# Chunked attention and expert layer on one core: two heads' key rows interleaved, memory values added by a product

## The chip, the core and the metric

The kernel runs on one core of one Trainium2 chip. The metric is the device time of one execution in microseconds (us), as the median of several runs. One execution is also recorded by the hardware profiler; all views of the profile below come from that one.

The core has a matrix engine (PE, which multiplies a loaded weight tile by a moving operand and writes into the accumulator memory, PSUM), a vector engine (DVE), a scalar engine (ACT), a general engine (POOL, which here also issues most of the DMAs) and a queue engine (SP, which only issues DMAs). The working memory has 128 partitions. The engines run on their own and wait for one another by semaphores.

## The reference

Two layers follow each other. The first is attention with a short window: batch 4, 8 heads, 768 positions, head size 64. The positions are cut into chunks of 32; each chunk sees its own 32 keys, 16 to the left and 8 to the right, so 56, and 8 memory keys that all chunks of a head share, 64 in all.

```python
for c in range(nc):
    q_c = q[:, :, c_start:c_end]
    k_full = np.concatenate([mem_k, k_ctx], axis=2)
    v_full = np.concatenate([mem_v, v_ctx], axis=2)
    scores = scale * np.matmul(q_c, k_full.transpose(0, 1, 3, 2))
    scores = scores - np.max(scores, axis=-1, keepdims=True)
    a = np.exp(scores)
    a = a / (np.sum(a, axis=-1, keepdims=True) + 1e-09)
    out[:, :, c_start:c_end] = np.matmul(a, v_full)
```

The second layer sends each of the 3072 resulting rows of 512 numbers to 2 of 8 experts, chosen by noisy logits (`x @ w_gate` plus noise scaled by a softplus of `x @ w_noise`). Each expert computes `np.maximum(x @ w1[e], 0) @ w2[e]` with a hidden width of 1024, and the two results are added with softmax weights.

## The kernel before

**Stages.** The attention works through the four batches one after the other. Within a batch it takes 256 queries at a time, two tiles of 128, so there are 3 iterations per batch and 12 in all (index i, or t in the helpers). Beside it, groups of finished rows are routed (the class `Route`: logits to choices, ranks and lists), and at the end the lists are decoded. Then comes the experts' stage: it gathers rows by pairs of experts and computes the expert layers in `mm1` (L697) and `mm2` (L709). The attention's working buffers (`xrow`, `vn`, `vb`, `nat`) lie in the place of experts' weights that are loaded later.

**Values' home.** `vb[b % 2]` holds, for each of the 24 chunks of a batch, the values that its queries see, in a layout for two heads at once. Partitions 0 to 63 belong to the even head of a pair: first its 8 memory rows, then its 56 key rows. Partitions 64 to 127 belong to the odd head in the same way. In the free direction there are two halves, `a = 0` for even heads and `a = 1` for odd heads. The even heads' partitions hold values in half 0 and zeros in half 1, the odd heads' the other way round, so that one product over 128 partitions gives both heads' results side by side. The zeros are written once: for `vb[1]` by ACT (L218), for `vb[0]` by DVE (L515).

How it is filled, per batch: the values `vn` (loaded by POOL, L117) are put in order by two POOL copies into `vp` (`spread_v`, L357). SP writes `vp` to the buffer `vd` in main memory (L363). POOL then issues six DMAs (`window_v`): two bring the 8 memory rows of the batch from `mvn` into the partitions of each head, copied for all 24 chunks (L367), and four bring the 56 key rows of each head, 32 and 24 rows at a time (L372). `mvn` comes from four SP loads of `mem_v` (L162) and a DVE cast (L516).

**An iteration.** `scores(i + 1)`: PE multiplies the queries by the memory keys (8 products over the whole array, L397) and by the windows' keys (32 products, each in one quarter of the array's columns, L404). DVE takes the maximum (L412) and subtracts it (L414); ACT takes the exponentials into `pb` (`exps`, L419). `turn_p(i)`: PE transposes `pb` in 8 pieces (L425), so that a pair of heads lies over the partitions with its 2 x 64 keys, and ACT copies the result to `pT` (L428). `turn_x(i - 1)`: PE transposes the finished rows (L459), ACT copies them (L461). `values(i)`: 8 products with the two columns of `ones2` give the sums of the exponentials (L436), into the PSUM tile `small`; 32 products in quarters of the array give the weighted values (L442), into `ps_o`. DVE takes the reciprocal of the sums (L446) and multiplies by it, once per tile of 128 queries (L449). `gate(i - 1)`: PE multiplies the transposed rows by the router's weights (L469), into other columns of `small`, and DVE copies the logits out (L471). Between these, `fill` transposes the next batch's keys and queries (L382) and copies them (L536); before the loop the same helper's copies for batch 0 are at L521.

**What sets the order.** The attention loop stands in a block of manual schedule for PE, ACT, DVE and SP: each engine works in the order in which the program writes its instructions. POOL's instructions keep their order by `pin`. So an instruction that waits holds back all that stands behind it on its engine. Waits are put in by the framework from the use of the tiles. PSUM is given out as three buffers that take turns for transposes (`psT`), one for `ps_s`, one for `ps_o` and one for `small`.

The loop's order, from the program:

```python
            if not last:
                sc = scores(i + 1)
            pTs[i] = turn_p(pbs.pop(i))
            if i:
                keep_x(i - 1, nc.scalar)
                xTs_[i - 1] = turn_x(xrs.pop(i - 1))
            fill(i, 1)
            xrs[i] = values(i, pTs.pop(i), (lambda: gate(i - 1, xTs_.pop(i - 1))) if last else None)
            if last:
                break
            pbs[i + 1] = exps(sc)
            ...
            if i:
                gate(i - 1, xTs_.pop(i - 1))
```

Of the kernel before, what the change touches and what calls it, by code (L numbers as in the profile page):

```python
# [22 lines left out]
def kernel(  # L23
# [29 lines left out]
    NCH = S // CH  # L53
# [6 lines left out]
    const = ctx.enter_context(tc.tile_pool(name="const", bufs=1))  # L60
# [3 lines left out]
    w_all = wpool.tile([128, E, WE], BF16, name="w_all")  # L64
# [5 lines left out]
    def pin(i):  # L70
        tc.keep_in_program_order(i)
# [23 lines left out]
    NP = len(pairs)  # L95
# [13 lines left out]
    vb = [scratch(2 * NCH * HP * D).rearrange("p (a c w) -> p a c w", a=2, c=NCH) for _ in range(2)][::-1]  # L109
    nat = [[scratch(H * SO * D).rearrange("p (h c) -> p h c", h=H) for _ in range(2)] for _ in range(2)]  # L110
    assert scol[0] >= 2 * WE
    mvs = w_all[0:B * NM, 0, 0:2 * H * D].bitcast(F32).rearrange("p (h d) -> p h d", h=H)

# [15 lines left out]
    actx = ExitStack()  # L129
# [5 lines left out]
    psO = actx.enter_context(tc.psum_pool(name="psO", bufs=1))  # L135
    psG = actx.enter_context(tc.psum_pool(name="psG", bufs=1))

# [22 lines left out]
    nc.vector.tensor_copy(mkn, mks)  # L160
    for b in range(B):
        nc.sync.dma_start(out=mvs[b * NM:(b + 1) * NM], in_=mem_v[b].rearrange("h m d -> m h d"))  # L162
    mvn = keep.tile([B * NM, Dm], BF16, name="mvn")
    wgs = keep.tile([128, KP, 2 * E], F32, name="wgs")
# [6 lines left out]
                   allow_small_or_imprecise_dtypes=True)  # L171

    ones2 = const.tile([128, 2], BF16, name="ones2")
    nc.vector.memset(ones2, 0.0)
    nc.vector.memset(ones2[0:64, 0:1], 1.0)
    nc.vector.memset(ones2[64:128, 1:2], 1.0)


# [20 lines left out]
    nc.gpsimd.iota(facts[:, :, 1], pattern=[[1, NG]], base=1, channel_multiplier=0, allow_small_or_imprecise_dtypes=True)  # L199

    ohp = const.tile([128, NG, NP], BF16, name="ohp")
    rank = const.tile([128, NG], F32, name="rank")
# [5 lines left out]
    def bc(ap, n):  # L208
        return ap.unsqueeze(len(ap.shape)).to_broadcast(list(ap.shape) + [n])

    def own(par):
        return slice(par * 64, par * 64 + 64)
# [4 lines left out]
    for par in range(2):  # L217
        nc.scalar.copy(vb[1][own(par), 1 - par].rearrange("p (x c) w -> p x (c w)", x=NCH // 2),  # L218
                       zeros[own(par), :].unsqueeze(1).to_broadcast([64, NCH // 2, Dm]))

# [140 lines left out]
    def window_v(b):  # L361
        t, o = vb[b % 2], vd[b % 2]
        nc.sync.dma_start(out=o[LC:LC + S, :].rearrange("(p s) c -> p (s c)", s=SO), in_=vp)  # L363
        for par in range(2):
            p0 = par * 64
            cols = slice(par * 256, (par + 1) * 256)
            pin(nc.gpsimd.dma_start(out=t[p0:p0 + NM, par], in_=mvn[b * NM:(b + 1) * NM, cols].unsqueeze(1).to_broadcast([NM, NCH, 256])))  # L367
        for par in range(2):
            p0 = par * 64
            cols = slice(par * 256, (par + 1) * 256)  # L370
            for r0, n in ((0, CH), (CH, WIN - CH)):
                pin(nc.gpsimd.dma_start(out=t[p0 + NM + r0:p0 + NM + r0 + n, par],  # L372
                                        in_=o[r0:r0 + S, cols].rearrange("(c k) w -> k c w", k=CH)[0:n]))

# [13 lines left out]

    small = psG.tile([128, 4, 128], F32, name="small")

# [26 lines left out]
    def exps(sc):  # L417
        pb = work.tile([128, 2 * HP, 2, KW], BF16, name="pb")
        nc.scalar.activation(out=pb.rearrange("p x a w -> p (x a) w"), in_=sc, func=Act.Exp, scale=scale)  # L419
        return pb  # L420

    def turn_p(pb):
        p_p = bank([128, 2 * HP, 128], BF16, name="p_p")
        for x in range(2 * HP):
            nc.tensor.transpose(out=p_p[:, x, :], in_=pb[:, x].rearrange("p a w -> p (a w)"),  # L425
                                identity=identb)
        pT = work.tile([128, 2 * HP, 128], BF16, name="pT")
        nc.scalar.copy(pT, p_p)  # L428
        return pT

    def values(t, pT, between=None):
        b, tp = divmod(t, TP)
        ps_g = small[:, t % 2, 0:2 * H].rearrange("p (j h) -> p j h", j=2)
        for x in range(2 * HP):
            j, pair = divmod(x, HP)
            nc.tensor.matmul(out=ps_g[:, j, 2 * pair:2 * pair + 2], lhsT=pT[:, x, :], rhs=ones2,  # L436
                             start=True, stop=True)
        ps_o = psO.tile([128, 2, HP, 2, D], F32, name="ps_o")
        for j in range(2):
            for pair in range(HP):  # L440
                for r in range(4):
                    nc.tensor.matmul(out=ps_o[r * CH:(r + 1) * CH, j, pair], lhsT=pT[:, j * HP + pair, r * CH:(r + 1) * CH],  # L442
                                     rhs=vb[b % 2][:, :, (tp * 2 + j) * 4 + r, pair * D:(pair + 1) * D],
                                     start=True, stop=True, tile_position=(0, r * CH))
        rs = work.tile([128, 2, H], F32, name="rs")
        nc.vector.reciprocal(rs, ps_g)  # L446
        xr = xrow[b % 2][:, 2 * tp:2 * tp + 2]
        for j in range(2):
            nc.vector.tensor_tensor(out=xr[:, j, 0:Dm].rearrange("p (h d) -> p h d", h=H),  # L449
                                    in0=ps_o[:, j].rearrange("p c a d -> p (c a) d"), in1=bc(rs[:, j], D), op=Alu.mult)  # L450
            if j == 0 and between is not None:
                between()
        return xr
# [10 lines left out]
    def gate(t, xT):  # L464
        b, tp = divmod(t, TP)
        ps_l = small[:, 2 + t % 2, 0:4 * E].rearrange("p (j e) -> p j e", j=2)
        for j in range(2):
            for kp in range(KP):
                nc.tensor.matmul(out=ps_l[:, j, :], lhsT=xT[:, kp, j, :], rhs=wgn[:, kp, :],  # L469
                                 start=(kp == 0), stop=(kp == KP - 1))  # L470
        nc.vector.tensor_copy(lg_all[:, 2 * t:2 * t + 2, :], ps_l)  # L471
# [34 lines left out]
    with tc.manual_schedule(engines={ET.PE, ET.Activation, ET.DVE, ET.SP}):  # L506
# [7 lines left out]
        for par in range(2):  # L514
            nc.vector.memset(vb[0][own(par), 1 - par], 0.0)  # L515
        nc.vector.tensor_copy(mvn.rearrange("m (a c d) -> m a c d", a=2, c=HP), mvs.rearrange("m (c a) d -> m a c d", a=2))  # L516
        spread_v(0)
# [9 lines left out]
        nc.vector.tensor_copy(wgn, wgs)  # L527
        pf = work.tile([128, 2, NP], F32, name="pf")
        sidon(pf, pab)
# [438 lines left out]
```

## Time and profile before

| what | value |
|---|---|
| median of 3 runs | 369.55 us (367.07 to 370.01) |
| profiled execution, its own time | 367.86 us |
| its span in the profile | 366.2 us |
| mean granted PE clock | 0.872 |
| PE, DVE, ACT, POOL busy | 282.3, 171.0, 136.7, 134.9 us |
| DMA moved | 56.97 MB in 55462 packets |
| vd windows, L372 | 8 DMAs of 384 KB, 8 of 288 KB |
| memory rows, L367 | 8 DMAs of 96 KB |

How to read the views: a line of a group or of a timeline has the start (timeline only), the busy time, the engine (PEld is PE's loading of weights), the program line, the operation, the tile written and, behind the arrow, the tiles read, and the shape; `x8` is the number of instructions that the line merges. In square brackets stands the idle time of the engine ahead of it and what ended that time; "issue" means that the profile shows nothing that it waited for. Buffers that lie in the experts' weights are all called `w_all` there. The windows view gives, for each stretch of time, its length, the busy time of each engine with the number of instructions, the granted PE clock as a share of full speed, the DMA share and GB/s. A POOL DMA line is the time to issue it, not to move its bytes.

### The profile page before, as it was taken

The page shows a single profiled execution, that of the slowest core. Times are in us where ns is not written, and L with a number is a line of the kernel's source. Part 1 is how long each engine was busy: PE and PEld are TensorE (multiplying, and loading weights), DVE is VectorE, ACT ScalarE, POOL GpSimd, SP SyncE. Part 2 cuts the span into 40 slices and gives each one's busy share as a digit, 9 for nine tenths or more (in the row PEclk, how much of TensorE's full clock was granted, in tenths as well). Part 3 has the DMA queues.
Part 4 walks back from the last instruction along what each step waited for, and adds up shares of the span by engine and source line. Part 5 has one row for each costly group of instructions (what it writes and reads, how often), then busy time and mean ns, then how long its engine had stood idle before and what let it go on. Part 6 is the DMA issues. An engine that isn't in the chain of part 4 may idle for free.

```text
span 366.2 us, 7045 instructions
## 1 busy us (share of the span) xinstructions
PE 282.3 (77%) x2941; PEld 181.3 (50%) x2941; DVE 171.0 (47%) x344; ACT 136.7 (37%) x189; POOL 134.9 (37%) x181
## 2 busy tenths in 40 slices
PE   0347373766817752599999999999989999999992
PEld 0236363555715641565554455764436675565540
DVE  7656274699766989431223300964300233312231
ACT  8714554463644360034333243222234223234310
POOL 6460473336435014742651453352480032201122
PEclk9995656685775885599999999999999999999997
DMA  8999999999999999379999999991299982100012
GB/s 115 247 155 169 248 162 155 258 199 199 237 176 198 228 225 180 80 147 179 159 186 206 250 184 240 101 215 54 69 154 186 193 185 80 52 2 2 24 43 81
DMA packets 55462, 56.97 MB, mean 156 GB/s; under 512 B 20119, under 2 KB 45783, under 8 KB 55424
## 3 DMA queue, kind: packets, MB, share of 16 engines
q0 software_dynamic: 34240, 46.82, 73.9%
q1 hardware_dynamic: 14048, 6.62, 9.5%
q10 hardware_dynamic: 7136, 3.02, 4.3%
q8 instruction: 25, 0.41, 0.5%
q14 instruction: 13, 0.11, 0.1%
HBM read 70.39 MB, written 13.96 MB: 230 GB/s over the span
## 4 chain that ended last, share of the span: by engine, by line
issue 25%; PE 21%; POOL 8%; DVE 5%; DMA 2%; POOLq 1%; ACT 0%; another core or an unknown queue 0%; DVEq 0%
PE p_h L697 10%; PE p_y L709 9%; POOL out_dram L660 6%; DMA out_dram<-y,main_dst 1%; POOL xt L654 1%; DMA xt<-xd,main_src 1%; PE p_xt L674 1%; DVE h L683 1%; POOL w_all L826 0%; DVE cum L322 0%; DVE w_all L449 0%; POOLq L963 0%; ACT xT L461 0%; DVE oh_l L328 0%
## 5 line engine op out<-in xcount | busy, mean ns | idle before, releaser
L709 PE MATMUL p_y<-w_all,h 128*128 128x512 bf16 x464 | 103.9, 379 | 1.5 <-ACT y L713 1.5
L697 PE MATMUL p_h<-xTt,w_all 128*128 128x256 bf16 (+3 forms) x672 | 102.9, 313 | 1.1 <-issue 0.5
L697 PEld LDWEIGHTS <-w_all 128*128 128x128 bf16 x736 | 69.8, 100 | 37.1 <-issue 1.6
L685 ACT ACTIVATE h<-p_h 128x512 bf16<-128x512 f32 (+1 forms) x81 | 44.5, 551 | 98.6 <-PE p_h L697 90.7
L709 PEld LDWEIGHTS <-h 128*128 128x128 bf16 x464 | 45.3, 98 | 53.2 <-issue 1.8
L683 DVE TENSOR_SCALAR h<-p_h 128x512 bf16<-128x512 f32 (+1 forms) x49 | 31.0, 632 | 85.9 <-PE p_h L697 70.5
L660 POOL DMA_INDIRECT out_dram<-y,main_dst x28 | 30.8, 1101 | 86.0 <-DVE y L715 75.6
L382 PE MATMUL p_t<-identb,w_all 128*64 128x128 bf16 x384 | 19.3, 272 | 30.8 <-DMA w_all<-in_k_dram 14.8
L715 DVE SCALAR_TENSOR_TENSOR y<-p_y,main_w,y 128x512 f32<-128x512 f32 x28 | 21.0, 750 | 37.9 <-PE p_y L709 33.3
L654 POOL DMA_INDIRECT xt<-xd,main_src x28 | 27.5, 982 | 26.3 <-DMA xTt<-xt 13.3
L713 ACT ACTIVATE y<-p_y,main_w 128x512 f32<-128x512 f32 x28 | 19.1, 687 | 38.8 <-PE p_y L709 35.6
L382 PEld LDWEIGHTS <-w_all 128*64 128x64 bf16 x384 | 16.4, 143 | 33.0 <-DMA w_all<-in_k_dram 15.5
L372 POOL DMA_DIRECT2D w_all<-vd x16 | 11.8, 745 | 26.4 <-DMA vd<-vp 25.3
L428 ACT COPY pT<-p_p 128x1024 bf16<-128x1024 bf16 x12 | 12.1, 1010 | 23.5 <-PE p_p L425 23.5
L449 DVE TENSOR_TENSOR w_all<-ps_o,rs 128x512 bf16<-128x512 f32 x24 | 15.5, 686 | 10.5 <-PE ps_o L442 10.0
L536 DVE COPY kT<-p_t 64x768 bf16<-64x768 bf16 x12 | 11.5, 955 | 12.5 <-PE p_t L382 12.4
L419 ACT ACTIVATE pb<-sc 128x1024 bf16<-128x1024 f32 x12 | 12.8, 1062 | 10.9 <-DVE sc L414 10.9
L357 POOL COPY vp<-w_all 128x1536 bf16<-128x1536 bf16 x8 | 11.5, 1467 | 13.3 <-DMA w_all<-in_v_dram 13.3
L442 PE MATMUL ps_o<-w_all,pT 128*32 128x128 bf16 x384 | 10.6, 274 | 6.1 <-issue 5.0
L412 DVE TENSOR_REDUCE mx<-ps_s 128x16 f32<-128x1024 f32 x12 | 14.7, 1223 | 1.2 <-PE ps_s L404 0.9
L414 DVE TENSOR_TENSOR sc<-ps_s,mx 128x1024 f32<-128x1024 f32 x12 | 14.7, 1224 | 0.8
L404 PE MATMUL ps_s<-kT,qT 128*32 128x112 bf16 x384 | 11.2, 274 | 3.6 <-DVE kT L536 2.4
(166 smaller groups left out, 279.3 us busy)
## 6 DMA issues: line engine op xcount, KB each, us to landing
w_all<-in_moe_w_dram POOLq DMA_DIRECT2D x16, 1024.0 KB
w_all<-in_moe_w_dram POOLq DMA_DIRECT2D x8, 512.0 KB
w_all<-in_v_dram POOLq DMA_DIRECT2D x4, 768.0 KB
w_all<-in_k_dram POOLq DMA_DIRECT2D x4, 768.0 KB
w_all<-in_q_dram POOLq DMA_DIRECT2D x4, 768.0 KB
vd<-vp SPq DMA_DIRECT2D x4, 768.0 KB, 6.9
w_all<-vd POOLq DMA_DIRECT2D x8, 384.0 KB
xd<-w_all ACTq DMA_DIRECT2D x11, 256.0 KB, 12.0
```

Of the source, the lines that this page charges most:

```text
L382: nc.tensor.transpose(out=p_t[own(par), s, :], in_=src[:, 2 * pair + par, s * D:(s + 1) * D], identity=identb, tile_position=(0, par * 64))
L412: nc.vector.tensor_reduce(out=mx, in_=s3, axis=AX, op=Alu.max)
L414: nc.vector.tensor_tensor(out=sc, in0=s3, in1=bc(mx, KW), op=Alu.subtract)
L449: nc.vector.tensor_tensor(out=xr[:, j, 0:Dm].rearrange("p (h d) -> p h d", h=H), in0=ps_o[:, j].rearrange("p c a d -> p (c a) d"), in1=bc( ...
L654: i = nc.gpsimd.indirect_dma_start(out=xts[key].bitcast(I32), out_offset=None, in_=xd, in_offset=bass.IndirectOffsetOnAxis(ap=ix, axis=0))
L660: i = nc.gpsimd.indirect_dma_start(out=out, out_offset=bass.IndirectOffsetOnAxis(ap=ix, axis=0), in_=y, in_offset=None, bounds_check=N - 1 ...
L683: nc.vector.tensor_scalar(out=out_, in0=in_, scalar1=0.0, scalar2=None, op0=Alu.max)
L685: nc.scalar.activation(out=out_, in_=in_, func=Act.Relu)
L697: nc.tensor.matmul(out=o, lhsT=w(kp * F + f * 128, 128), rhs=x[:, kp], start=(kp == 0), stop=(kp == KP - 1))
L709: nc.tensor.matmul(out=p, lhsT=h[:, (f * n + j) * 128:(f * n + j + 1) * 128], rhs=w(KP * F + f * Dm, Dm), start=(f == 0), stop=(f == FB - 1))
L713: nc.scalar.activation(out=y, in_=p, func=Act.Copy, scale=weight)
L715: nc.vector.scalar_tensor_tensor(out=y, in0=p, scalar=weight, in1=y, op0=Alu.mult, op1=Alu.add)
```

## The change

- In `vb`, the key rows of the two heads of a pair alternate: row r of the even head lies in partition 2 (8 + r), that of the odd head in the partition behind it. The exponentials `pb` are written with the heads alternating as well, so the transposed `pT` has the same order.
- The memory rows are no longer copied into `vb`. Its partitions 0 to 15 stay zero; so both halves of `vb` are zeroed over all 128 partitions.
- A new tile `mvz` holds, for each batch and pair, the memory values of both heads in partitions 0 to 15 (zeros below), 64 columns and a 65th per head; the 65th column is one in the partitions of the own head. Eight POOL DMAs fill it from `mem_v` at the start.
- In `values`, the product for the sums becomes a product with `mvz`, of 130 columns: it gives the memory part of both heads' results and the sums. The four window products of the same pair follow at once and add to it, so products over the whole array and in quarters of it alternate eight times.
- The PSUM tiles `ps_o` and `small` become one tile `prods` of 1536 columns. The parts of the two tiles of queries start at columns 0 and 703, the gate's results lie from 1408 on.
- The reciprocal is taken once per tile of 128 queries, ahead of each multiply.

```diff
-    mvs = w_all[0:B * NM, 0, 0:2 * H * D].bitcast(F32).rearrange("p (h d) -> p h d", h=H)
-    psG = actx.enter_context(tc.psum_pool(name="psG", bufs=1))
...
-    for b in range(B):
-        nc.sync.dma_start(out=mvs[b * NM:(b + 1) * NM], in_=mem_v[b].rearrange("h m d -> m h d"))
-    mvn = keep.tile([B * NM, Dm], BF16, name="mvn")
+    mvz = keep.tile([128, B, HP, 2, D + 1], BF16, name="mvz")
+    nc.vector.memset(mvz, 0.0)
...
-    ones2 = const.tile([128, 2], BF16, name="ones2")
...
+    for par in range(2):
+        for b in range(B):
+            pin(nc.gpsimd.dma_start(out=mvz[par:2 * NM:2, b, :, par, 0:D],
+                                    in_=mem_v[b].rearrange("(c a) m d -> a m c d", a=2)[par]))
...
-        nc.scalar.copy(vb[1][own(par), 1 - par].rearrange("p (x c) w -> p x (c w)", x=NCH // 2),
-                       zeros[own(par), :].unsqueeze(1).to_broadcast([64, NCH // 2, Dm]))
+        nc.scalar.copy(vb[1][:, par].rearrange("p (x c) w -> p x (c w)", x=NCH // 2),
+                       zeros.unsqueeze(1).to_broadcast([128, NCH // 2, Dm]))
...
-        for par in range(2):
-            p0 = par * 64
-            cols = slice(par * 256, (par + 1) * 256)
-            pin(nc.gpsimd.dma_start(out=t[p0:p0 + NM, par], in_=mvn[b * NM:(b + 1) * NM, cols].unsqueeze(1).to_broadcast([NM, NCH, 256])))
         for par in range(2):
-            p0 = par * 64
-            cols = slice(par * 256, (par + 1) * 256)
             for r0, n in ((0, CH), (CH, WIN - CH)):
-                pin(nc.gpsimd.dma_start(out=t[p0 + NM + r0:p0 + NM + r0 + n, par],
-                                        in_=o[r0:r0 + S, cols].rearrange("(c k) w -> k c w", k=CH)[0:n]))
+                p0 = 2 * (NM + r0) + par
+                pin(nc.gpsimd.dma_start(out=t[p0:p0 + 2 * n - 1:2, par],
+                                        in_=o[r0:r0 + S, par * 256:(par + 1) * 256].rearrange("(c k) w -> k c w", k=CH)[0:n]))
...
-    small = psG.tile([128, 4, 128], F32, name="small")
+    prods = psO.tile([128, 1536], F32, name="prods")
+
+    def prod(j):
+        return prods[:, j * 703:j * 703 + 764].rearrange("p (c w) -> p c w", w=191)[:, :, 0:2 * (D + 1)]
+
+    def heads(j):
+        return prod(j).rearrange("p c (a d) -> p c a d", a=2)
...
-        pb = work.tile([128, 2 * HP, 2, KW], BF16, name="pb")
-        nc.scalar.activation(out=pb.rearrange("p x a w -> p (x a) w"), in_=sc, func=Act.Exp, scale=scale)
+        pb = work.tile([128, 2 * HP, KW, 2], BF16, name="pb")
+        nc.scalar.activation(out=pb.rearrange("p x w a -> p x a w"), in_=sc.rearrange("p (x a) w -> p x a w", a=2), func=Act.Exp, scale=scale)
...
-        ps_g = small[:, t % 2, 0:2 * H].rearrange("p (j h) -> p j h", j=2)
         for x in range(2 * HP):
             j, pair = divmod(x, HP)
-            nc.tensor.matmul(out=ps_g[:, j, 2 * pair:2 * pair + 2], lhsT=pT[:, x, :], rhs=ones2,
-                             start=True, stop=True)
-        ps_o = psO.tile([128, 2, HP, 2, D], F32, name="ps_o")
-        for j in range(2):
-            for pair in range(HP):
-                for r in range(4):
-                    nc.tensor.matmul(out=ps_o[r * CH:(r + 1) * CH, j, pair], lhsT=pT[:, j * HP + pair, r * CH:(r + 1) * CH],
-                                     rhs=vb[b % 2][:, :, (tp * 2 + j) * 4 + r, pair * D:(pair + 1) * D],
-                                     start=True, stop=True, tile_position=(0, r * CH))
-        rs = work.tile([128, 2, H], F32, name="rs")
-        nc.vector.reciprocal(rs, ps_g)
+            nc.tensor.matmul(out=prod(j)[:, pair], lhsT=pT[:, x, :], rhs=mvz[:, b, pair].rearrange("p a d -> p (a d)"),
+                             start=True, stop=False)
+            for r in range(4):
+                nc.tensor.matmul(out=heads(j)[r * CH:(r + 1) * CH, pair, :, 0:D], lhsT=pT[:, x, r * CH:(r + 1) * CH],
+                                 rhs=vb[b % 2][:, :, (tp * 2 + j) * 4 + r, pair * D:(pair + 1) * D],
+                                 start=False, stop=True, tile_position=(0, r * CH))
+        rs = work.tile([128, 2, HP, 2], F32, name="rs")
         xr = xrow[b % 2][:, 2 * tp:2 * tp + 2]
         for j in range(2):
-            nc.vector.tensor_tensor(out=xr[:, j, 0:Dm].rearrange("p (h d) -> p h d", h=H),
-                                    in0=ps_o[:, j].rearrange("p c a d -> p (c a) d"), in1=bc(rs[:, j], D), op=Alu.mult)
+            nc.vector.reciprocal(rs[:, j], heads(j)[:, :, :, D])
+            nc.vector.tensor_tensor(out=xr[:, j, 0:Dm].rearrange("p (c a d) -> p c a d", c=HP, a=2),
+                                    in0=heads(j)[:, :, :, 0:D], in1=bc(rs[:, j], D), op=Alu.mult)
             if j == 0 and between is not None:
                 between()
...
-        ps_l = small[:, 2 + t % 2, 0:4 * E].rearrange("p (j e) -> p j e", j=2)
+        ps_l = prods[:, 1408 + t % 2 * 4 * E:1408 + (t % 2 + 1) * 4 * E].rearrange("p (j e) -> p j e", j=2)
...
-            nc.vector.memset(vb[0][own(par), 1 - par], 0.0)
-        nc.vector.tensor_copy(mvn.rearrange("m (a c d) -> m a c d", a=2, c=HP), mvs.rearrange("m (c a) d -> m a c d", a=2))
+            nc.vector.memset(vb[0][:, par], 0.0)
+        odd = route.tile([128, 2], F32, name="odd")
+        nc.vector.tensor_reduce(out=odd, in_=identb.rearrange("p (m a) -> p a m", a=2), axis=AX, op=Alu.add)
+        nc.vector.tensor_copy(mvz[:, :, :, :, D].rearrange("p b c a -> p (b c) a"),
+                              odd.unsqueeze(1).to_broadcast([128, B * HP, 2]))
...
-        pf = work.tile([128, 2, NP], F32, name="pf")
+        pf = route.tile([128, 2, NP], F32, name="pf")
```

More of the change, by code (lines that the diff above doesn't have):

```diff
@@ L171 @@
                    allow_small_or_imprecise_dtypes=True)
-    ones2 = const.tile([128, 2], BF16, name="ones2")
-    nc.vector.memset(ones2, 0.0)
-    nc.vector.memset(ones2[0:64, 0:1], 1.0)
-    nc.vector.memset(ones2[64:128, 1:2], 1.0)
     tri = const.tile([128, 128], BF16, name="tri")
@@ L424, in turn_p @@
         for x in range(2 * HP):
-            nc.tensor.transpose(out=p_p[:, x, :], in_=pb[:, x].rearrange("p a w -> p (a w)"),
+            nc.tensor.transpose(out=p_p[:, x, :], in_=pb[:, x].rearrange("p w a -> p (w a)"),
                                 identity=identb)
```

## The prediction

> **What bounds the kernel now.** I read the page first: its span, and the slices of the busy time. Then the windows view over three stretches. Then, for the first stretch, the timelines of PE, DVE and POOL.
>
> ```profile
> span 366.2 us, 7045 instructions
> ...
> PE   0347373766817752599999999999989999999992
> ...
> DMA  8999999999999999379999999991299982100012
> ```
>
> ```profile
> 28.00:135.00 107.00, 64.65 (x1508) 54.25 (x1506) 73.96 (x138) 53.54 (x65) 38.53 (x50) 0.69 1.22 205
> ...
> 150.00:366.00 216.00, 206.19 (x1249) 117.64 (x1249) 65.75 (x126) 64.42 (x111) 73.16 (x75) 0.97 0.71 129
> ```
>
> A slice is 9.15 us and a digit its busy tenths: DMA is full in nearly every slice to 155 us, PE only behind that. From 150 us on, PE is busy 206 of 216 us: the experts' stage is PE's, and the change does not touch it. It only starts later or earlier, one for one. In the attention stage no engine is full: DVE has 74 of 107 us, PE 65, at a granted clock of 0.69, while DMA is full. So the chain of waits inside an iteration decides. PE's timeline shows one iteration, and then a second block of the same kind at the full clock:
>
> ```profile
> 54.00 0.37 PE L436 MATMUL small<-ones,pT 128*128 128x2 bf16 x8 [0.31 <-ACT pT L428]
> 54.30 1.05 PE L442 MATMUL ps_o<-w_all,pT 128*32 128x128 bf16 x32
> 55.28 0.38 PE L469 MATMUL small<-wgn,xT 128*128 128x16 bf16 x8
> 55.52 0.36 PE L397 MATMUL ps_s<-mkT,qT 128*128 128x16 bf16 x8
> 55.81 0.94 PE L404 MATMUL ps_s<-kT,qT 128*32 128x112 bf16 x32
> 56.67 1.03 PE L425 MATMUL p_p<-identb,pb 128*128 128x128 bf16 x8
> 57.50 0.71 PE L459 MATMUL p_x<-identb,w_all 128*128 128x128 bf16 x8
> 58.87 0.35 PE L436 MATMUL small<-ones,pT 128*128 128x2 bf16 x8 [0.66 <-ACT pT L428]
> 64.20 1.10 PE L442 MATMUL ps_o<-w_all,pT 128*32 128x128 bf16 x32 [4.98 <-issue]
> ...
> 87.06 0.36 PE L469 MATMUL small<-wgn,xT 128*128 128x16 bf16 x8 [2.38 <-DVE rs L446]
> ...
> 98.80 0.35 PE L436 MATMUL small<-ones,pT 128*128 128x2 bf16 x8
> 99.08 0.63 PE L442 MATMUL ps_o<-w_all,pT 128*32 128x128 bf16 x32
> 99.64 0.36 PE L469 MATMUL small<-wgn,xT 128*128 128x16 bf16 x8
> ...
> 102.74 1.14 PE L382 MATMUL p_t<-identb,w_all 128*64 128x128 bf16 x34 [1.95 <-DMA w_all<-in_k_dram]
> 111.11 0.96 PE L382 MATMUL p_t<-identb,w_all 128*64 128x128 bf16 x14 [7.23 <-issue]
> ```
>
> An undisturbed iteration runs from 54.00 to 58.87, 4.9 us, and PE hardly pauses in it. The 4.98 us at 64.20 come where the next batch's windows (L372) are first used, so I read them as their arrival. PE's other waits for transfers in this timeline are 1.11 (L442 at 32.46), 3.64, 0.70 and 1.95 (k), 2.58 and 1.12 us (q); all seven make 16.1 us. The 7.23 us at 111.11 fall inside a row of transposes that nothing else interrupts; the page has a queue for instructions, so I take it for late code.
>
> **The change part by part.** The sum stands against the profiled execution: 367.86 us, 1.7 around its span, 1.7 under the median of 369.55.
>
> *PE: sums become products, alternating with the windows.* Before, eight 2-column products run in a block (0.30 us), then 32 window products in quarters of the array (0.98): 1.28 us; at 98.80 the same takes 0.28 + 0.56 = 0.84. After, each of eight steps has one 130-column product and four window products. Four terms make a step:
> - the 130 columns: nearest is L425, eight of 128 columns in 0.83 us (56.67 to 57.50), 0.104 each; fast 0.058 (95.36 to 95.82);
> - from the whole array to quarters: L469 starts eight in 0.24 (0.03 each), so the block at 54.00 has 0.30 - 7 x 0.03 = 0.09 between its last start and the first quarter;
> - four window products together: L404 takes 0.59 us for 20 (51.22 to 51.81) and 0.86 for 32, so 0.09 for four and 0.14 at the end, before the whole array works again; fast, 0.36 for 20 (80.49) and 0.51 for 32 (119.61), 0.05 and 0.11. For L442 this leaves (0.98 - 0.14) / 8 = 0.105, fast 0.056;
> - from quarters to the whole array: those 0.14 or 0.11.
>
> A step is 0.44 us slow, 0.31 fast; eight are 3.5 and 2.5. The growth is 2.2 or 1.7 us. At a mean clock of 0.69 I take 2.0; twelve iterations: **+24 us**. The bounds are 12 x 2.2 = 26 above, and below only the columns (0.077 slow, 0.03 fast per step, 5.8 us in all) if the switches hide. That a window product adds to what the product left: L469 adds four times into the same columns at 0.03 us, so nothing.
>
> The window products now write two runs of 64 columns, 65 apart. L404 writes two runs of 56, 64 apart, at 0.09 us per 112 columns; L442, in one run, 0.105 per 128: no price, so none in the sum. The Trainium skill, "PSUM — Partial Sum Buffer", Specifications, says that any non-contiguous pattern slows matmuls significantly; L404's row does not bear it out, though no row has a run at an odd column. Taken as twice the window time, an estimate from the rows, it would add 0.105 x 8 x 12 = 10 us, 396 in all.
>
> *PE waits for DVE.* Gate (L469) sits in PE's order right behind the windows. At 87.06 it waited for rs (L446), which reads other columns of the tile `small`: accesses to one PSUM tile stand in line. After, gate writes into `prods`, the tile that both reciprocals and both multiplies read, so it waits for all four. That tail: two reciprocals of 8 values (rows: 0.25 for 16, 0.17 to 0.20 for 6 to 8 elements), two multiplies (0.69), with hand-overs 1.9 us, where gate now follows at once. Queued behind gate on PE are scores, turn_p, turn_x and the next values, so the iteration grows by it. Gate waits in iterations 1 to 10 (the eleventh waits for one multiply only): 19 us, less the 1.81, 2.38 and 2.01 us that it stood in three of them already, 12.8, plus 0.5 for the last: **+13.3**. The bounds: 0 if dependencies go by columns, 19.5.
>
> *Transfers.* The memory rows leave the queue: 192 of 1536 KB per batch (from the page's sizes). v(2) landed at 52.33 by POOL's timeline and the windows at 64.20: 11.9 us, so 1.5 per batch by bytes. The windows' rows go to other partitions, same sizes. But PE arrives later now, by about 2 us at batch 1 and over 10 at batch 3, so it finds everything there: all **-16.1**, whatever the queue does. This is the most that the transfers can give.
>
> *The late code.* PE reaches that place some 12 us later, still beside expert loads; I take half of 7.23: **-3.6**, bounds -7.2 and +3 (a second one).
>
> *The start.* POOL's timeline:
>
> ```profile
> 6.53 0.24 POOL L199 IOTA facts<- 128x24 bf16 x1
> 9.48 2.87 POOL L357 COPY vp<-w_all 128x1536 bf16<-128x1536 bf16 x2 [2.71 <-DMA w_all<-in_v_dram]
> 13.57 1.36 POOL L367 DMA_DIRECT2D w_all<-mvn  x2 [1.22 <-DVE mvn L516]
> 19.56 2.95 POOL L372 DMA_DIRECT2D w_all<-vd  x4 [4.63 <-DMA vd<-vp]
> ```
>
> Eight mvz loads at L367's 0.68 take 5.4 us, 2.7 of them in the idle time. The vp copy, SP's vd write behind it and the first windows start up to 2.7 later; their queue is 1.5 shorter and q and k finish earlier beside it. I take **+0.5**, bounds -1 and +2.7.
>
> *At nothing.* The removed L367 issues: POOL idles for vd behind each. vb's memsets (2.62) and ACT's zeroing (5.31) get twice the partitions, no more columns: kT's 64x768 copy takes 0.955, qT's 128x768 0.958. mvz's memset (by columns 0.9), its sums' columns and the `odd` reduce: DVE idles 2.1 us before 15.39; without that, 1.2. SP's four mem_v issues and mvn's cast (0.41) gain nothing there. The exponentials (1.06) write in steps: even doubled they end long before turn_p, which comes 4 us later. The multiplies read with gaps: L412 and L414 take 1.22 for 1024 elements, L536's permuted copy 0.955 for 768, 4% more each, so 0.03. `pf` changes pools only.
>
> Sum: 367.9 + 24 + 13.3 - 16.1 - 3.6 + 0.5 = **386**.
>
> **The rivals.**
> - *Gate is not held.* Dependencies go by columns. For: nothing in the trace; against: 87.06. 386 - 13.3 = 373.
> - *Odd runs cost*, above: 396.
> - *Faster: transfers are the bound and switches hide.* The place is the DMA queue of batches 1 to 3, full in every slice there. If the windows ran at the rate of the k load (768 KB from 70.88 to 75.65, 4.8 us), their 1344 KB would take 8.4 instead of 10.4 us; with the memory rows 3.5 per batch, 10.5 in three. With only the columns' 5.8 us on PE: 363. It decides when PE's growth stays below 10.5 / 12 = 0.9 us an iteration; against it, the switches stand in the rows at both clocks. The Trainium skill, "SBUF — State Buffer", Door 1, says that partitions 0 to 63 reach 8 of 16 DMA ports; rows interleaved over both halves would then move up to twice as fast, all 16.1 us would go, and this rival would give 358. No view here shows ports.
> - *No difference.* Only the memory rows' 4.5 us and the columns' 5.8: 369.
>
> **How the numbers follow.** The forecast has 0.64, gate not held 0.10, odd runs 0.07, faster 0.13, no difference 0.06. With the bounds of its terms the forecast alone reaches from 377 (all blocks fast, code stall gone, start -1) to 403 (all slow, gate's tail whole, a second stall, start +2.7); ends that need all four together I leave out. The range 370 to 399 leaves out the faster rival, about half of no difference and that upper tip. Faster by over 1% (what a measurement here tells from no change) 0.13; within 1%: no difference and half of gate not held, 0.11; slower 0.76.
>
> **What would show it.** Right: in PE's timeline products and windows alternate at 0.44 or 0.31 us a step, gate waits 1.9 us for DVE's multiply, and no L382 or window product waits for DMA from batch 2 on. Wrong: the eight steps end within 2 us, gate follows at once, or PE still stands for q, k or vd. The experts' stage should still take 216 us; if not, the sum misses a part.

## The result, and the profile after

The changed kernel took 411.37 us (median of 4 runs, 408.15 to 411.95), the kernel before 369.78 beside it (367.07 to 370.67): a ratio of 1.115, 95% interval 1.109 to 1.120. It is slower, as forecast, but by 42 us and not by 18, and outside the range.

The page after, the lines that answer to those shown of before:

```profile
span 410.1 us, 7031 instructions
...
PE   0247307767858587742899999999998999999993
...
DMA  9869999595099991100498999996217995110012
```

A slice is now 10.25 us. DMA, full in nearly every slice of the attention stage before, has holes: 0 in the eleventh slice, 1, 1, 0, 0 from the sixteenth. The queue is no longer what the stage is short of. The windows view over the attention and the experts' stage:

```profile
28.00:135.00 107.00, 63.91 (x1049) 46.15 (x1042) 50.88 (x95) 40.01 (x44) 32.32 (x39) 0.66 0.97 180
...
195.00:410.00 215.00, 203.99 (x1224) 116.65 (x1244) 65.74 (x126) 64.42 (x111) 72.27 (x74) 0.98 0.65 129
```

In the same 107 us PE does 1049 matmuls where it did 1508, DVE 95 instructions where it did 138. The experts' first product starts at 195.4 us where it started at 151.4, 44.0 us later, which is the whole difference of the two spans: the loss is all ahead of the experts' stage, as forecast. PE's timeline after: the router's product of the first group, one group of the first batch at the lower clock, one of the second batch at the full clock:

```profile
61.81 0.38 PE L462 MATMUL prods<-wgn,xT 128*128 128x16 bf16 x8 [16.94 <-ACT xT L454]
...
72.83 0.29 PE L432 MATMUL prods<-mvz,pT 128*128 128x130 bf16 x1 [0.30 <-ACT pT L425]
73.05 0.30 PE L435 MATMUL prods<-w_all,pT 128*32 128x128 bf16 x4
73.28 0.29 PE L432 MATMUL prods<-mvz,pT 128*128 128x130 bf16 x1
...
93.72 0.23 PE L432 MATMUL prods<-mvz,pT 128*128 128x130 bf16 x1
93.88 0.24 PE L435 MATMUL prods<-w_all,pT 128*32 128x128 bf16 x4
94.06 0.23 PE L432 MATMUL prods<-mvz,pT 128*128 128x130 bf16 x1
```

The steps are 0.45 us slow (72.83 to 73.28) and 0.34 fast (93.72 to 94.06), against 0.44 and 0.31 in the prediction. New is the first line: PE stands 16.94 us in the router's product, and not for DVE but for ACT's xT. PE's waits and then ACT's, after (from waiting line to awaited work; us in all, times, longest):

```profile
PE prods L462 <- ACT xT L454: 27.3, 4, 16.9
PE prods L462 <- DVE w_all L442: 12.3, 8, 1.9
PE p_t L373 <- DMA w_all<-in_k_dram: 7.7, 1, 7.7
```

```profile
ACT xT L454 <- DMA w_all<-vd: 32.4, 3, 18.7
```

The same waits before, of the router's product and of xT; none of ACT's was for windows:

```profile
PE small L469 <- DVE rs L446: 4.6, 3, 2.4
PE small L469 <- ACT xT L461: 2.9, 2, 1.8
```

```profile
ACT xT L461 <- PE p_x L459: 2.1, 1, 2.1
ACT xT L461 <- DVE rs L446: 1.8, 1, 1.8
```

And ACT's timeline at the same place:

```profile
60.33 0.38 ACTq L469 DMA_DIRECT2D xd<-w_all  x1
60.74 1.01 ACT L454 COPY xT<-p_x 128x1024 bf16<-128x1024 bf16 x1 [18.66 <-DMA w_all<-vd]
61.65 1.45 ACT L416 ACTIVATE pb<-sc 128x1024 bf16<-128x1024 f32 x1
```

Take the second line first. xT is copied out of PSUM and needs no window. It stands behind L469 (`keep_x`, L476 before), ACT's store of the finished attention rows, which was issued only at 60.33, once the next batch's windows (`w_all<-vd`, L363) had landed. Three times ACT stands so, 32.4 us in all: at the first store behind the issue of the next batch's windows (stores at 60.33, 88.03 and 123.52, of groups 0, 2 and 5); behind the store are xT, the exponentials, the next batch's copies, and PE.

The third thing is the start, on POOL:

```profile
6.63 3.35 POOL L194 DMA_DIRECT2D mvz<-in_mem_v_dram  x6
13.28 0.54 POOL L194 DMA_DIRECT2D mvz<-in_mem_v_dram  x1 [3.29 <-DMA w_all<-in_k_dram]
17.08 0.54 POOL L194 DMA_DIRECT2D mvz<-in_mem_v_dram  x1 [3.26 <-DMA w_all<-in_q_dram]
17.62 2.88 POOL L353 COPY vp<-w_all 128x1536 bf16<-128x1536 bf16 x2
24.36 3.02 POOL L363 DMA_DIRECT2D w_all<-vd  x4 [3.86 <-DMA vd<-vp]
```

The last two memory loads wait for the k and q loads, and the values' copy behind them starts at 17.62 and not at 9.48. DVE waits for the same loads, ahead of the first batch's kT copies (before, then after):

```profile
15.39 3.90 DVE L521 COPY kT<-p_t 64x768 bf16<-64x768 bf16 x4 [2.11 <-PE p_t L382]
```

```profile
19.35 1.24 DVE L511 CAST mvz<-odd 128x32 bf16<-128x32 f32 x1 [4.50 <-DMA mvz<-in_mem_v_dram]
20.61 3.88 DVE L517 COPY kT<-p_t 64x768 bf16<-64x768 bf16 x4
```

L511 writes the ones into `mvz` and comes only once the loads into that tile have landed; the kT copies stand behind it.

### The profile page after: what moved, and what is told of

It reads as the page before. It is cut to its first block, busy times and chain, and to the rows that moved or that the text cites. A ratio compares the mean times of both kernels' runs of the same rounds, so it can differ in the third digit from the quotient of the medians.

```text
span 410.1 us, 7031 instructions
## 1 busy us (share of the span) xinstructions
PE 313.3 (76%) x2920; PEld 196.3 (48%) x2941; DVE 173.9 (42%) x355; ACT 139.9 (34%) x189; POOL 134.2 (33%) x181
## 4 chain that ended last, share of the span: by engine, by line
PE 32%; issue 26%; DMA 16%; POOL 11%; DVE 9%; ACT 3%; POOLq 1%; ACTq 0%; DVEq 0%
PE p_h L693 10%; PE p_y L705 8%; DMA w_all<-vd 7%; POOL out_dram L656 6%; PE prods L435 3%; DMA w_all<-in_q_dram 3%; PE prods L432 3%; DMA w_all<-in_v_dram 3%; POOL w_all L363 2%; DVE kT L532 2%; DVE w_all L442 2%; PE p_t L373 2%; PE p_p L422 2%; PE ps_s L401 1%; ACT pT L425 1%
## 5 line engine op out<-in xcount | busy, mean ns | idle before, releaser
L705 PE MATMUL p_y<-w_all,h 128*128 128x512 bf16 x446 | 102.5, 379 | 2.5 <-ACT y L709 1.6
L650 POOL DMA_INDIRECT xt<-xd,main_src x28 | 27.4, 980 | 25.9 <-DMA xTt<-xt 14.5
L462 PE MATMUL prods<-wgn,xT 128*128 128x16 bf16 x96 | 4.4, 174 | 39.7 <-ACT xT L454 27.3
L373 PE MATMUL p_t<-identb,w_all 128*64 128x128 bf16 x384 | 21.2, 293 | 17.0 <-DMA w_all<-in_k_dram 7.7
L432 PE MATMUL prods<-mvz,pT 128*128 128x130 bf16 x96 | 25.6, 267 | 3.9 <-ACT pT L425 3.7
L373 PEld LDWEIGHTS <-w_all 128*64 128x64 bf16 x384 | 18.7, 159 | 18.9 <-issue 10.3
L435 PE MATMUL prods<-w_all,pT 128*32 128x128 bf16 x384 | 26.4, 266 | 0.5 <-DMA w_all<-vd 0.5
L454 ACT COPY xT<-p_x 128x1024 bf16<-128x1024 bf16 x12 | 12.2, 1016 | 38.3 <-DMA w_all<-vd 32.4
L462 PEld LDWEIGHTS <-xT 128*128 128x128 bf16 x96 | 4.1, 104 | 41.0 <-ACT xT L454 28.1
L363 POOL DMA_DIRECT2D w_all<-vd x16 | 12.1, 761 | 26.3 <-PE prods L435 16.5
L416 ACT ACTIVATE pb<-sc 128x1024 bf16<-128x1024 f32 x12 | 16.4, 1367 | 6.8 <-DVE sc L411 6.8
L353 POOL COPY vp<-w_all 128x1536 bf16<-128x1536 bf16 x8 | 11.5, 1468 | 21.8 <-DMA w_all<-vd 13.1
L441 DVE RECIPROCAL rs<-prods 128x8 f32<-128x8 f32 x24 | 4.9, 203 | 29.8 <-PE prods L435 29.8
```

Of the source, the lines that this page charges most:

```text
L363: pin(nc.gpsimd.dma_start(out=t[p0:p0 + 2 * n - 1:2, par], in_=o[r0:r0 + S, par * 256:(par + 1) * 256].rearrange("(c k) w -> k c w", k=CH) ...
L373: nc.tensor.transpose(out=p_t[own(par), s, :], in_=src[:, 2 * pair + par, s * D:(s + 1) * D], identity=identb, tile_position=(0, par * 64))
L432: nc.tensor.matmul(out=prod(j)[:, pair], lhsT=pT[:, x, :], rhs=mvz[:, b, pair].rearrange("p a d -> p (a d)"), start=True, stop=False)
L435: nc.tensor.matmul(out=heads(j)[r * CH:(r + 1) * CH, pair, :, 0:D], lhsT=pT[:, x, r * CH:(r + 1) * CH], rhs=vb[b % 2][:, :, (tp * 2 + j) * ...
L650: i = nc.gpsimd.indirect_dma_start(out=xts[key].bitcast(I32), out_offset=None, in_=xd, in_offset=bass.IndirectOffsetOnAxis(ap=ix, axis=0))
L705: nc.tensor.matmul(out=p, lhsT=h[:, (f * n + j) * 128:(f * n + j + 1) * 128], rhs=w(KP * F + f * Dm, Dm), start=(f == 0), stop=(f == FB - 1))
```

## The experiments

**Theory A**, from the trace: the store's wait is made by the program, which takes the windows, since they are written with a step of two over the partitions, for an overlap with the rows that the store reads. They lie in the same tile `w_all`, but nowhere on the same bytes. The rest of the loss would be the products': switching, the router's wait for DVE, the start. **Rival B**: the wait is real and moves elsewhere. **Rival C**: the layout costs nothing, the products nearly all. Rivals D to H and V come up below. All ratios are to the kernel before, run beside each, with 95% intervals; 0.01 is about 3.7 us.

**1. view16.** The store reads the same bytes as 16-bit and not as 32-bit numbers.

```diff
-        q.dma_start(out=xd[g0 * 128:(g0 + 2) * 128, :].rearrange("(s p) r -> p s r", p=128),
-                    in_=xrow[b % 2][:, 2 * tp:2 * tp + 2].bitcast(I32))
+        q.dma_start(out=xd[g0 * 128:(g0 + 2) * 128, :].bitcast(BF16).rearrange("(s p) r -> p s r", p=128),
+                    in_=xrow[b % 2][:, 2 * tp:2 * tp + 2])
```

> The changed kernel with one edit: ScalarE's store of the attention rows reads them through their own 16-bit type and not through a 32-bit view of the same bytes; addresses and bytes stay. Theory A (the wait is the program's own: written with a step of two over the partitions, the windows are taken for an overlap with the rows that this view reads): ScalarE's copy of the turned rows loses its 32.4 us of idle time behind the windows' transfers and TensorE's router product most of its 27.3 us behind ScalarE; 411.4 goes to 380 to 392. Rival B (the rows or the queues really need the windows' transfers, so the wait shows up at the next instruction): over 405.

Measured: 390.16 us, 1.065 (1.058 to 1.072); the changed kernel stood at 1.115. ACT no longer waits for windows at all, and PE's first wait is another one:

```profile
PE prods L462 <- DVE w_all L442: 18.4, 11, 1.9
PE p_t L373 <- DMA w_all<-in_k_dram: 7.7, 1, 7.7
PE p_t L373 <- DVE kT L517: 6.6, 2, 6.3
```

One view of the same bytes is worth 0.050, some 18 us. Rival B falls: the wait does not turn up at another instruction of ACT, nor at PE, which waits 0.5 us for windows as in the changed kernel. Part of the 27.3 us that PE stood for ACT does come back as PE's wait for DVE, 18.4 us and not 12.3.

**2. views.** POOL's copy of the values had the same wait (L353, 13.1 us in the changed kernel). Taken one head at a time it has none.

```diff
-        for par in range(2):
+        for h in range(H):
             pin(nc.gpsimd.tensor_copy(
-                out=vp.rearrange("p (s a c d) -> p a c s d", s=SO, a=2, c=HP)[:, par],
-                in_=vn.rearrange("p (c a) (s d) -> p a c s d", a=2, s=SO)[:, par]))
+                out=vp.rearrange("p (s a c d) -> p c a s d", s=SO, a=2, c=HP)[:, h // 2, h % 2],
+                in_=vn[:, h].rearrange("p (s d) -> p s d", s=SO)))
```

> As view16, and GpSimd's copy of the values takes one head at a time (eight copies of 128x384 and not two of 128x1536), a view that the program does not order behind the windows. Theory A: GpSimd's 13.1 us of waits for the windows' transfers vanish, the store of the values and the next windows go out earlier, and 2 to 8 us come on top of view16: 375 to 388. Rival B: as view16 or slower, since the eight copies cost more than two.

Measured: 389.41 us, 1.062 (1.055 to 1.069): no difference to view16 that can be told. POOL's wait was beside the path; I had expected 2 to 8 us.

**3. layout_only, 4. halves.** One part of the change each. layout_only is the kernel before with interleaved rows: the windows' and the memory rows' targets and the exponentials' tile as in the change, `ones2` from `odd`, sums and fetched memory rows kept. halves is the changed kernel with the old homes; shown is the windows' target, and the targets of `mvz`, the tile `pb` and the ones' partitions follow it:

```diff
-                p0 = 2 * (NM + r0) + par
-                pin(nc.gpsimd.dma_start(out=t[p0:p0 + 2 * n - 1:2, par],
+                p0 = par * 64 + NM + r0
+                pin(nc.gpsimd.dma_start(out=t[p0:p0 + n, par],
...
```

> The kernel before with the interleaved rows alone: windows and memory rows with a step of two, exponentials written so, the sums' two columns for even and odd rows; memory rows still fetched into the home, sums and no products. Theory A: the new wait of ScalarE's store comes with the layout and not with the products; 369.8 goes to 385 to 400. Rival C (the loss is the products': switching and the router's wait are larger than my sum had them): 367 to 373.

> The changed kernel with the old homes: one head's rows in partitions 0 to 63, the other's in 64 to 127, products kept, memory rows still added by them. Theory A: no pattern has a step of two, ScalarE and GpSimd wait for no windows, time as in views, 375 to 388. Rival C: 400 or more, since the products are all there.

Measured: layout_only 387.31 us, 1.056 (1.049 to 1.063); halves 390.90 us, 1.066 (1.059 to 1.073). ACT's waits in layout_only:

```profile
ACT xT L459 <- DMA w_all<-vd: 44.6, 3, 20.3
```

The wait comes with the layout, without any product. And products without the layout cost 24 us. For halves theory A's 375 to 388 was too low. Each part alone costs over 20 us. Neither halves, which has the 32-bit view and no step of two, nor view16, which has the step and not the view, shows a wait of ACT for windows: it takes both. How the program comes to order them so, no trace shows.

**5. gate_first, 6. grouped, 7. late_memory, 8. all_three.** The products' parts one by one, on top of views. gate_first forms the router's product ahead of DVE's scaling:

```diff
+        ps_l = None if gated is None else gate_sums(*gated)
         rs = work.tile([128, 2, HP, 2], F32, name="rs")
...
+        if gated is not None:
+            nc.vector.tensor_copy(lg_all[:, 2 * t - 2:2 * t, :], ps_l)
```

grouped lets the eight products of a group run ahead of its 32 window products, with `start` at the first product of each bank:

```diff
-                             start=True, stop=False)
+                             start=x in (0, 3, 6), stop=False)
+        for x in range(2 * HP):
+            j, pair = divmod(x, HP)
             for r in range(4):
...
-                                 start=False, stop=True, tile_position=(0, r * CH))
+                                 start=False, stop=x in (2, 5, 7), tile_position=(0, r * CH))
```

late_memory leaves two of the eight memory loads ahead of the values' copy and puts six behind `load_v(2)`.

> On top of views (389.4, 23.2 over the kernel before): TensorE forms the router's product straight behind the window products, ahead of VectorE's two reciprocals and two multiplies, which then wait for it. Theory A (what is left is the products' own: the router's wait, the switching, the start): the 18.0 us in eleven waits behind VectorE's multiplies shrink to under 3, VectorE pays some 0.4 us a group: 371 to 379. Rival D (the tail on VectorE is on the path either way, since the transposes of its rows and the next scores wait for it too): 385 or more.

> On top of views: the eight products of a group in a row, then its 32 window products, so TensorE changes between the whole array and quarters once and not eight times a group. Theory A: by my terms seven pairs of 0.23 (slow) or 0.17 (fast) us go, 17 us in twelve groups: 369 to 376. Rival D (switching is beside other waits, or costs less than the rows made me think): 383 or more.

> On top of views: of the eight loads of memory values only the first batch's two stand ahead of the copy of the first values, six come behind the third batch's value load. Theory A: the copy starts where it did before (9.5 us and not 17.6), the first window product some 3 us earlier: 384 to 388. Rival D: the first groups wait for something else next (VectorE's kT copies, ScalarE): 388 to 391.

> views with gate_first, grouped and late_memory together. Theory A: the three add up, 389 less 14, 17 and 3 gives 355, 11 under the kernel before; allowed 350 to 361. Rival D (TensorE's savings turn into waits for the transfers of k, q and the windows, which the kernel before had for 21 us): 363 to 372.

Measured: gate_first 377.27 us, 1.022 (1.015 to 1.029), 0.040 or 14.5 us under views. grouped 374.47 us, 1.015 (1.009 to 1.022), 17 us under views. late_memory 391.59 us, 1.062 (1.055 to 1.069), no difference to views that can be told, where 1.4 to 5.4 us were expected. all_three 361.90 us, 0.981 (0.974 to 0.988): faster than the kernel before, between the two expectations. grouped's timeline, one group slow:

```profile
58.29 1.05 PE L432 MATMUL prods<-mvz,pT 128*128 128x130 bf16 x8 [0.31 <-ACT pT L425]
59.28 0.83 PE L437 MATMUL prods<-w_all,pT 128*32 128x128 bf16 x32
62.00 0.34 PE L464 MATMUL prods<-wgn,xT 128*128 128x16 bf16 x8 [1.89 <-DVE w_all L444]
```

Products and windows take 1.8 us here where the eight alternating steps took 8 x 0.45 = 3.6. The router's wait stays; it is gate_first's.

In late_memory the first window product does come early (31.32 and not 36.48), and the experts' first product too (172.0 and not 177.5, from the traces). Then the experts' stage takes 207.5 us from first to last product, where in views it took 204.2. That is not late_memory's doing. In all seven traces of runs whose kernel before stood at 366.2 the stage takes 203.8 to 204.8 us and PE never pauses over 0.2 us in it; in the ten others, whose kernel before stood at 369.2 to 369.8, it takes 207.4 to 207.7, with the same pauses, the longest of 1.4 to 1.7 us for ACT's y. So it goes with the group of runs and not with the edit; what makes it is not known. Each against its own kernel before, late_memory is 22.4 us over and views 23.2, and the intervals are too wide to tell a gain of some 3 us from none.

**9. layout_views, 10. views_gate_grouped, 11. halves_gate_grouped, 12. before_gate_first.** What is the layout worth without its wait? layout_views is layout_only with both views; views_gate_grouped is all_three without late_memory; halves_gate_grouped the same in the old homes; before_gate_first the kernel before with the router's product first.

> layout_only with the two views of view16 and views: the interleaved rows without the waits that they brought, sums and fetched memory rows as in the kernel before. Theory A: the whole loss of layout_only (1.056 of the kernel before) was those waits: 0.99 to 1.01 of it. Rival F (rows that lie over all partitions move faster, so the transfers' waits shrink): 0.985 or less, 5 us or more faster. Rival G (interleaving costs in itself, by the stepped exponentials or the copies): 1.015 or more.

> all_three without late_memory: the two views, the router's product first, products grouped. Theory A: 0.98 to 0.99 of the kernel before, since late_memory alone was worth nothing in the end; with it, all_three was 0.981. Rival D: the start counts once the rest is gone: 0.99 to 1.0.

> The old homes (halves) with products, the router's product first, products grouped: views_gate_grouped without the interleaving. Theory A: as views_gate_grouped within 1%, since the homes matter only through the waits. Rival F (interleaved rows move faster): 1% or more slower than views_gate_grouped. Rival G: 1% or more faster.

> The kernel before with one edit: the router's product straight behind the window products, ahead of VectorE's scaling. It stood 4.6 us for VectorE and 2.9 us for ScalarE there. Theory A: 0.985 to 1.0 of the kernel before, so most of all_three's gain over it is not this edit's alone. Rival H (all of the gain is this edit): 0.98 or less.

Measured: layout_views 356.66 us, 0.966 (0.962 to 0.969): rival F, and theory A's 0.99 to 1.01 is wrong. views_gate_grouped 365.56 us, 0.988 (0.984 to 0.991). halves_gate_grouped 369.71 us, 1.002 (0.999 to 1.005): interleaving is worth 0.014 here too (the two views are missing there as well; run 13 shows that without interleaving they give nothing). all_three, the same with late_memory, had 0.981: 2.4 us less, but the intervals overlap. before_gate_first 369.18 us, 0.996 (0.992 to 1.000).

In layout_views PE's seven waits for transfers in the loop, 16.1 us before, are five of 8.5 us, and the 7.2 us taken for late code are 3.3: 11.5 of the 13 us. The trace's records of single packets show the transfers themselves. The value and memory rows of the attention stage come in packets of 4096 bytes, 384 per batch in both kernels; by batch, from the first packet's start to the last one's:

| | median ns of a packet | us from first to last |
|---|---|---|
| before | 379, 460, 374, 370 | 12.6, 15.0, 11.4, 15.4 |
| layout_views | 274, 266, 298, 262 | 10.7, 9.4, 9.7, 10.8 |

Same bytes, same packets, some 30% less time each, 14 us less in the sum of the four batches. In the kernels with products, which move 336 such packets per batch, that sum is 34.8 to 37.6 us interleaved and 43.5 and 44.9 in the old homes. The Trainium skill, "SBUF — State Buffer", Door 1 and "Can I just issue two DMAs to hit both halves?", says that partitions 0 to 63 and 64 to 127 lie on different halves of 16 ports, that one transfer uses the ports of its own span, and that two transfers on the two halves serialize. The packets agree in direction; no run here shows the ports. And the halves alone do not explain it: a window transfer of 32 rows now reaches from partition 16 to 79, but one of 24 rows from 80 to 127, within one half as before (40 to 63 or 104 to 127). The last 72 packets of each batch, as many as such a transfer has, took 438 to 682 ns in the median before and 207 to 311 in layout_views. Why the packets are shorter stays open.

**13. before_views, 14. layout_view16, 15. layout_views_gate.** layout_views differs from the kernel before in the two views as well. So: these alone, the layout with the store's view alone, and the layout with the router's product first.

> The kernel before with the two views alone (store through the 16-bit type, values copied one head at a time), old homes. Theory F (the 3.4% of layout_views are the interleaved rows', whose packets moved in less time): 0.99 to 1.01 of the kernel before. Rival V (they are the views'; the copies or the store leave earlier): 0.975 or less.

> layout_views without the copies one head at a time: the store alone is mended. Theory F: GpSimd's copies wait for the windows again (14.7 us in layout_only) but little hangs on it: 0.965 to 0.98 of the kernel before. Rival: the next windows start late for it, 0.99 or more.

> layout_views with the router's product ahead of VectorE's scaling: the version that the runs so far point to. TensorE stood 2.3 us for VectorE and 2.6 for ScalarE there in the router's product. Theory F: 0.955 to 0.97 of the kernel before. Rival: as before_gate_first, no difference that can be told, and it stays at 0.966.

Measured: before_views 366.63 us, 1.001 (0.998 to 1.004), packets at 375 to 497 ns: the views give nothing, rival V falls. layout_view16 354.22 us, 0.968 (0.964 to 0.972). layout_views_gate 353.60 us, 0.967 (0.963 to 0.971), no difference to layout_views that can be told. The page of layout_view16:

```profile
span 354.6 us, 7044 instructions
...
PE   0347577575756723999999999999999999999991
...
DMA  8979999999899994498999999961399961100012
...
q0 software_dynamic: 34240, 46.82, 71.1%
```

The last line is the queue's: 34240 packets, 46.82 MB, as in the kernel before, but 71.1% of 354.6 us (252) where that had 73.9% of 366.2 (271).

So half of the change with one view mended is the best version, 3.2% under the kernel before; it is the simplest of three that can't be told apart. Against layout_only, that view is worth 0.088 or 32 us.

## Why the prediction came out as it did

Direction and most of the sum's rows were right; the time was missed mainly because of one wait that the sum does not have. The steps, the router's waits behind DVE and the vanished waits of PE for windows, q and k came out as the prediction's signs of being right had them; none of these signs looked at ACT.

- **The step that failed** is "Transfers": "The windows' rows go to other partitions, same sizes". It priced bytes and asked only PE's waits for q, k and windows. It did not ask who else waits for a DMA once its pattern changes. ACT's store (L476 in the kernel before) got a wait for the next windows, and with it all that is queued on ACT behind it. view16 puts it at 18 us in the changed kernel; layout_only against layout_view16 at 32 where no product hides part of it. Without it the changed kernel is 24 us over the kernel before (0.065 of 369.8), 394 or so, inside the range; the sum had 18.
- **"all -16.1, whatever the queue does"**: in the changed kernel these waits of PE are gone, as forecast; 7.7 us for k and 0.5 for windows at the start remain. What "same sizes" left out is that interleaving makes the transfers themselves shorter: layout_views, with a PE that is not slowed, is 13 us faster by it, still under the 16.1 that the term set as the most. In the changed kernel a PE that arrives late hides that. The faster rival had shorter transfers, with 358 for rows "over both halves", and it was given 0.13 in all. The shorter transfers were real, the store's wait and the products covered them; the halves cannot be the whole reason, since the 24-row transfers stay in one.
- **Switching, +24**: steps of 0.45 and 0.34 us were forecast within 0.03. Grouping, priced at 17 us from the same terms, gave 17.
- **The router's wait, +13.3**: waits of up to 1.9 us, eight of them in the changed kernel and eleven in view16 (18.4 us, against 4.6 before: 13.8). gate_first gave 14.5. "Gate is not held" falls. Whether the whole tile holds the product back or only the part of it that both use, no run separates.
- **Odd runs, a rival at 396**: falls. The windows with gaps are in the steps above, which kept to the forecast without a price for them.
- **The late code, -3.6**: the whole 7.23 us went in the changed kernel, and with a faster PE some of it is back (3.3 us in layout_views' waits). Its cause was not tried.
- **The start, +0.5**: mis-sized, and on another path. The sum counted POOL's issues. The first window product comes 3.0 us later (32.46 to 35.44), beyond the bound of +2.7, but PE waits only 0.51 us for the windows there. The delay is DVE's, which the prediction had at nothing: the ones in `mvz` wait 4.50 us for the loads, the kT copies behind them start at 20.61 and not at 15.39, PE stands 6.2 us for one, and the first scores start at 25.96 and not at 22.89. late_memory takes the delay away (22.80); its worth cannot be told from the noise.

For view16 the terms as now known are 24 + 13.8 - 16.1 - 7.2 + 3.1 (first window product at 35.55), 18 us of the 24 measured. Another 4 are PE's waits for DVE's kT (6.2 us against 2.4 before); some 2 us stay open. With the store's 18 that makes 40 of the changed kernel's 42. For halves they are 24 + 13.4 (the router's wait is 18.0 us there) - 16.1 - 7.2 + 4 (first window product at 36.8), also 18 of 24; another 2 are the waits for kT (4.5 us), and some 4 us stay open.

## What to carry to other kernels

When a transfer gets a new pattern, list the waits of every instruction that touches its tile, on all queues, and look first at what stands behind a store on a busy engine: a wait can come from a view of bytes that nobody shares. Rows that the matmul takes from two halves of the partitions can be worth interleaving, 3.4% here, for shorter transfers and not for shorter products. Products that use the whole array are kept together, away from those in quarters. And a small product that shares a PSUM tile with others goes ahead of the scaling that reads the tile where it waits for it: 14.5 us on top of views, where it waited 18, and nothing that can be told in the kernel before, where it waited 4.6.

## What the runs showed of the hardware

- Packets of 4096 bytes into every second partition took 262 to 298 ns in the median of a batch, into consecutive partitions 370 to 460 (layout_views and the kernel before; before_views, with the same views as layout_views, 375 to 497). In the kernels with products the medians are 299 to 360 and 347 to 414.
- Changing between the whole array and quarters cost 17 us in 84 changes and back (12 groups of seven), 0.2 us each, by grouped against views.
- POOL issues eleven DMAs in a row at the start: v, k, q and eight memory loads. The tenth waited 3.3 us for the second (k) and the eleventh 3.3 us for the third (q), eight places back, whose bytes they do not touch.
- Exponentials written in steps of two took 1.36 us and not 1.06 for 128x1024; in the changed kernel no product of PE waited for them.
